# A routed-attention and SwiGLU kernel: the fifth head group's transposition moves from TensorE to VectorE, with loads and mask rows reordered

## The chip, the core and the metric

The kernel runs on one core of a Trainium2 chip. A core has TensorE (matrix products, written PE in the profile, its weight loads PEld), VectorE (DVE), ScalarE (ACT), GpSimd (POOL) and SyncE (SP), which here only issues DMA transfers. Each engine works through its own list of instructions in order and waits for the others by semaphores. Engines compute on SBUF, the on-chip memory of 128 partitions; TensorE writes to PSUM[...]. The metric is the device time of one execution in microseconds (us), the median of several runs.

## The reference

Inputs are q, k and v of shape (4 batches, 8 heads, 768 rows, 64), 16 centroids per head, and the weights of a gated feed-forward layer (512 to 1536 to 512), all in float32.

```python
q_assign = argmax(normalized(q) @ normalized(centroids).T)     # the cluster of each q row
k_assign = argmax(normalized(k) @ normalized(centroids).T)
mask = q_assign[:, :, :, None] == k_assign[:, :, None, :]
scores = where(mask, q @ k.T / sqrt(64), -1e9)
attn = softmax(scores)
x = (attn @ v) put together over heads                         # 3072 rows of 512
xn = x / sqrt(mean(x * x) + 1e-6) * rms_g
g, val = xn @ w_gate, xn @ w_val
out = (silu(g) * val) @ w_out
```

## The kernel before

**Mask inside the product.** The mask is never built. Each q and k row is extended from 64 to 80 numbers: 64 of data and 16 that are one at the row's own cluster and zero elsewhere (with a factor `ZS` = 2048 between data and mask). The product of two extended rows is then large where the clusters agree, and one exponential with an offset (`off`) does scale and mask together. The tiles `qext` and `kext` hold the extended rows with the 80 numbers on partitions; there are four of each, one per head group in flight.

**Groups and units.** The 32 heads (batch times head) are cut into eight *groups* of four heads (`HG`), group g being heads 4g to 4g + 3. The 3072 rows of attention and feed-forward are cut into eight *units* of 384 rows, two for each batch. Unit u attends over the two groups of its batch: units 0 and 1 use groups 0 and 1, units 2 and 3 groups 2 and 3, and so on. One unit has 8 heads times 3 steps, 24 *gaps*: in each, TensorE makes two score products (`s`, L345) and ScalarE exponentiates them into `pT` (L349). One step later TensorE multiplies `pT` with v into `acc` (L363), and for every second head VectorE divides (L368, L370) into `x`. There is a single `acc` bank.

**What is filled in between.** Behind the score products of each gap, `attention` pulls items from a list `fill` by weights that stand for their TensorE time, so that they are spread evenly over the gaps. In unit u the list holds: the last eight products of the gated layer of unit u - 2; the normalization of unit u - 1 (`rms`), with the DMA transposition of `xn` to `xnT` (L403, on the SP queue); the output rows of unit u - 2 (`o`, L466, 3 rows of three parts, stored from `o_sb` tiles); the preparation of group u + 2 (`group_work`); and the first sixteen products `gate` and `val` (L441) of unit u - 1, followed by Tanh on ScalarE (L449) and two VectorE operations (L450, L454). In unit 1 two groups are prepared, 2 and 3.

**Preparing a group.** For each head: q and k are loaded (L85 or L93) into one of six `qk` stage buffers, transposed so that the 64 numbers lie on partitions (`trans`, into `qkT`, three tiles of two heads), cast to bf16 into `qext` and `kext` (`cast`, L237), and v is loaded into one of eight `vs` buffers and cast to `vbf` on GpSimd (L240). Then, once for q and once for k of the whole group (`cluster_steps`): products with the centroids (`sc`, L251), a VectorE transposition (`scT`), maximum, comparison (`ohT`) and transposition back (`oh`). `place` (L294) then copies the mask rows of `oh` into partitions 64 to 79 of `qext` and `kext` with 16 small DMAs, eight for q, eight for k.

**Two ways to transpose.** The constant `BG` decides. For groups below `BG`, a load is one DMA of 192 KB, whole rows; TensorE transposes (`tq`, L218, three for each of q and k of a head), ScalarE evicts from PSUM (L224), and `kext` is cast by VectorE. For groups from `BG` on, a load of q or k is four DMAs of 48 KB, half rows of 32 numbers (128 bytes), put down so that 32x32 blocks turned in place give the whole transposition; VectorE does it in one instruction (L214) and `kext` is cast by GpSimd. There the factor `ZS` goes into the mask rows of k (L282) instead of k itself.

**Queues.** The order on each engine is the order in which the program emits, set by the code (no scheduler moves it). SP issues loads, x transpositions, stores and, for group 2, the mask rows, and stands still when the next one has to wait. GpSimd issues the weight loads (`wg`, `wv`, `wo`) and the mask rows of groups 3 to 7 between its casts. The loads of head n + `NQ` (6) and of v for head n + `NV` (8) are emitted by `others`, behind the v cast of head n.

Of the kernel before, what the change touches and what calls it, by code (L numbers as in the profile page):

```python
# [9 lines left out]
F32 = mybir.dt.float32  # L10
# [12 lines left out]
def kernel(  # L23
# [12 lines left out]
    nc = tc.nc  # L36
    B, H, S, D = q.shape
# [3 lines left out]
    P = 128  # L41
    ST = S // P
    HT = ST // 2
    UQ = HT * P
    HG = 4
# [8 lines left out]
    CUT = 2 * FC - 8  # L54
    LEAD = 6
    NQ, NV = 6, 8
    BG = 5

    ctx.enter_context(tc.manual_schedule())
    pool = lambda n, b, **kw: ctx.enter_context(tc.tile_pool(name=n, bufs=b, **kw))  # L60
# [7 lines left out]
    gate = pool("gate", 3)  # L68
    outp = pool("outp", 3)
# [7 lines left out]
    def src(a, n):  # L77
        b, h = divmod(n, H)
        return a[b, h].rearrange("(p t) d -> p t d", t=ST)

    def load(n, part, on=None):
        if n not in staged:
            staged[n] = stage.tile([P, 2, ST, D], F32, tag="qk", name="qk")
        if n < BG * HG:
            (on or nc.sync).dma_start(out=staged[n][:, part], in_=src((q, k)[part], n))  # L85
            return

        to = staged[n][:, part].rearrange("p t d -> p (t d)").rearrange("p (i r d) -> p i r d", i=HT, d=32)
        of = (q, k)[part][n // H, n % H].rearrange("(r p i e) (c d) -> e c p i r d", p=32, i=HT, e=2, d=32)
        for e in range(2):  # L90
            for c in range(2):
                r = 32 * (2 * e + c)
                nc.sync.dma_start(out=to[r:r + 32], in_=of[e, c])  # L93

    def load_qk(n):
        if n < B * H:
            load(n, 0)
            load(n, 1)

    def load_v(n, vq=None):  # L100
        if n >= B * H:
            return
        stagedv[n] = stage.tile([P, ST, D], F32, tag="vs", name="vs", bufs=NV)
        (vq or nc.sync).dma_start(out=stagedv[n], in_=src(v, n))
# [104 lines left out]
    def trans(g, h, part, on=None):  # L209
        if (g, h // 2) not in qkT:  # L210
            qkT[g, h // 2] = qk32.tile([P, 2, 2, UQ], F32, tag="qkT", name="qkT")
        qk = staged[g * HG + h]
        if g >= BG:
            nc.vector.transpose(qkT[g, h // 2][:, h % 2, part], qk[:, part].rearrange("p t d -> p (t d)"))  # L214
            return
        ps = ps_g.tile([P, UQ], F32, tag="gen", name="tq")
        for i in range(HT):
            nc.tensor.transpose(ps[:, i * P:(i + 1) * P], qk[:, part, 2 * i:2 * i + 2].rearrange("p t d -> p (t d)"),  # L218
                                ident_f)
        to, by = qkT[g, h // 2][:, h % 2, part], 1.0 / ZS if part else 1.0  # L220
        if on is nc.vector:
            nc.vector.tensor_scalar_mul(to, ps, by)  # L222
        else:
            nc.scalar.activation(to, ps, ACT.Copy, scale=by)  # L224
# [5 lines left out]
    def cast(on, g, h, part, es=(0, 1)):  # L230
        for e in es:
            to = cols((kext if part else qext)[g % 4][:D, h], g, e)
            of = qkT[g, h // 2][e * D:(e + 1) * D, h % 2, part]
            if on is nc.scalar:
                nc.scalar.copy(to, of)
            else:
                on.tensor_copy(to, of)  # L237

    def vcast(n):
        nc.gpsimd.tensor_copy(vbf[n // HG % 4][:, n % HG, :, :D], stagedv[n])  # L240
# [24 lines left out]
    def cluster_steps(g, m):  # L265
# [13 lines left out]
        def back():  # L279
            put[g, m] = asg.tile([P, UQ], BF16, tag="oh", name="oh", bufs=3)  # L280
            if m and g >= BG:
                nc.vector.tensor_scalar_mul(of["ohT"], of["ohT"], ZS)  # L282
# [6 lines left out]
    def place(on, g, m, es=(0, 1)):  # L289

        ext = (kext if m else qext)[g % 4]
        for h in range(HG):
            for e in es:
                on.dma_start(out=ext[D:D + NC, h, e * UQ:(e + 1) * UQ],  # L294
                             in_=put[g, m][32 * h + e * NC:32 * h + (e + 1) * NC])
# [39 lines left out]
    def scores(u, h, i):  # L335
# [12 lines left out]
        of = ps[:, :, :w] if nt == HT else flat[:, :n * w].rearrange("p (c w) -> p c w", w=w)  # L348
        nc.scalar.activation(pT[u, h][:, n * i:n * i + n, :w], of, ACT.Exp, bias=off, scale=scale if g >= BG else scale * ZS)  # L349

# [107 lines left out]
    def out_rows(u, t):  # L458
        b, col, _ = UNITS[u]
        return out[b * S:(b + 1) * S].rearrange("(p t) f -> p t f", t=ST)[:, (col + t) % HT * 2 + (col + t) // HT]  # L460
# [11 lines left out]
    def out_part(u, t, i):  # L472

        c = slice(*((0, DM // 2), (DM // 2, DM * 3 // 4), (DM * 3 // 4, DM))[i])
        to = ps_g.tile([P, c.stop - c.start], F32, tag="gen", name="o")
        for f in range(FC):
            nc.tensor.matmul(to, lhsT=gvT[u][:, f, t * P:(t + 1) * P], rhs=wo[:, f, c], start=f == 0, stop=f == FC - 1)  # L477
        o = outp.tile([P, c.stop - c.start], F32, tag="o_sb", name="o_sb")
        if i == 1:
            nc.vector.tensor_copy(o, to)  # L480
        else:
            nc.scalar.copy(o, to)
        nc.sync.dma_start(out=out_rows(u, t)[:, c], in_=o)


    def group_work(g):

        t, c = [], []
        for h in range(HG):
            n = g * HG + h  # L490
            w = 0.0 if g >= BG else 0.3
            t += [(w, lambda h=h: trans(g, h, 0)), (w, lambda h=h: trans(g, h, 1))]

            def others(n=n):
                vcast(n)
                load_qk(n + NQ)
                load_v(n + NV)

            def both(h=h, f=others):
                cast(nc.gpsimd, g, h, 0)  # L500
                f()
                cast(nc.gpsimd if g >= BG else nc.vector, g, h, 1, (0,))
            if g == 2:
                c.append((0.0, others))
            else:
                c += [(0.0, both), (0.0, lambda h=h: cast(nc.gpsimd if g >= BG else nc.vector, g, h, 1, (1,)))]
        a = []
        for m in range(2):
            a += [(0.0 if i else 0.7, f) for i, f in enumerate(cluster_steps(g, m))]
            if g == 3:  # L510
                a.append((0.0, lambda m=m: place(nc.gpsimd, g, m)))
            elif g == 2:
                a.append((0.0, (lambda: (place(nc.sync, g, 1), place(nc.sync, g, 0, (1,)))) if m else
                          (lambda: place(nc.sync, g, 0, (0,)))))
        if g > 3:
            a[:1] = [(1.4, lambda f=(a[0][1], a.pop(4)[1]): [x() for x in f])]
            a.append((0.0, lambda: [place(nc.gpsimd, g, m) for m in range(2)]))
        return t, c, a
# [5 lines left out]
    def group(g):  # L524

        if g >= NG:
            return [], []
        t, c, a = group_work(g)
        return [x for h in range(HG) for x in t[2 * h:2 * h + 2] + c[2 * h:2 * h + 2]], a
# [77 lines left out]
    def second_batch():  # L607
        nc.sync.dma_start(out=hold, in_=invs[0].rearrange("p a t -> p (a t)"))
        for n in range(H + HG, H + NQ):
            load_qk(n)  # L610
        for n in range(H, H + NV):
            load_v(n)

    def gap1():
# [61 lines left out]
    for u in range(1, NU):  # L676
        ffn, o, g = ffn_work(u - 1), out_work(u - 2) if u > 1 else [], u + 2
        if u == 1:
            t, c, a = group_work(2)
            t3, c3, a3 = group_work(3)  # L680
            n = LEAD - 4
            o3 = [(0.0, lambda i=i: load_o(i)) for i in range(0, FC, 4)]
            prep = c + a + spread(weave(t3[n:], c3), o3) + a3[:5]
            idle = const.tile([P, 1], BF16)

            def norm():
                rms(0)
                nc.gpsimd.tensor_copy(idle, xn[0][:, CC - 1, HT - 1, P - 1:])
                for h in range(HG):
                    casts(pool_, H + h, K0, Q0, K1, Q1)  # L690

            hooks = {(1, 0, 0): late[6], (1, 0, 1): lambda: (late[7](), norm())}
            hooks.update({(1, *divmod(2 + i, HT)): t3[i][1] for i in range(n)})
            hooks[1, *divmod(LEAD - 1, HT)] = lambda: xtrans_all(0)
            fill = spread(ffn[:CUT], prep)
            attention([(1, h) for h in range(H)], fill, LEAD, hooks)
        else:
            fill = ffn_work(u - 2)[CUT:] + [(0.0, lambda u=u: rms(u - 1))]
            rows, clusters = group(g)
            if u == 2:  # L700
                fill += spread(o[:3], [(0.0, f) for _, f in a3[5:]])
                o = o[3:]
            fill += spread(o, rows) + spread(ffn[:CUT], clusters)
            attention([(u, h) for h in range(H)], fill, 1 if g < NG else 0)
# [41 lines left out]
```

The softmax here doesn't subtract the row's maximum and nothing guards it: scores larger than these inputs give would overflow.

## Time and profile before

| | |
|---|---|
| time, median of 3 runs | 333.88 us (333.72 to 334.36) |
| span of the profiled run | 331.7 us |
| score products `s`, L345 | 384, mean 328 ns |
| `gate` and `val`, L441 | 384 each, mean 326 ns |
| output products `o`, L466 | 276, mean 379 ns |
| TensorE transpositions `tq`, L218 | 120, mean 277 ns |
| exponentials, L349 | 192, mean 904 ns |
| VectorE transpositions `qkT`, L214 | 24, mean 544 ns |
| small q and k loads, L93 | 96 of 48 KB, median 2.7 us to landing |
| large q and k loads, L85 | 38 of 192 KB, medians 4.1 and 4.2 us to landing |

The profile is of one execution. A page gives the busy time of each engine, the chain of work that ended last, and groups of instructions by line; the trace behind it gives waits (who waited for whom: total, times, longest) and timelines (start, duration, engine, line, what; an idle time before and its releaser in brackets). Matmuls overlap, so a group's durations add up to more than the time that it takes; the distance from start to start shows that time. TensorE's clock was granted in full all through.

### The profile page before, as it was taken

Reading aid. Unit: us, or ns where it says so; the run is one execution under the profiler, and the core shown is the slowest. Engines: PE = TensorE matmul, PEld = TensorE weight load, DVE = VectorE, ACT = ScalarE, POOL = GpSimd, SP = SyncE. Lnnn points to the kernel's source line nnn. Section 1 sums busy time; section 2 is a strip of 40 time slices with the busy share of each in tenths; the row PEclk is TensorE's granted clock in tenths of the full one; section 3 lists DMA queues with packets and bytes.
Section 4 is the critical chain, followed back from the end, with each engine's and each line's share of the span. In section 5 each row is a group of like instructions: output and inputs, shape, how many; then the busy total and the mean of one; then the engine's idle time right before and its main releaser. Section 6 shows DMA issues by size and latency. Waiting matters only on the chain.

```text
span 331.7 us, 7838 instructions
## 1 busy us (share of the span) xinstructions
PE 323.6 (98%) x2901; PEld 195.4 (59%) x2901; DVE 222.1 (67%) x507; ACT 250.5 (76%) x437; POOL 124.7 (38%) x249
## 2 busy tenths in 40 slices
PE   8999899999999999999999999999999999999996
PEld 4647557565656655665556655665566656655654
DVE  6999876868378694877678694876355644685430
ACT  5899979976878877798768876798788868863322
POOL 6999498240926338260834438270000000000000
PEclk9999999999999999999999999999999999999999
DMA  8999988956755625561550022000400040002002
GB/s 272 374 262 203 244 161 224 204 152 127 154 118 98 146 55 117 118 137 34 90 139 26 14 60 85 3 21 4 121 24 1 2 109 35 2 1 77 20 0 97
DMA packets 71269, 34.23 MB, mean 103 GB/s; under 512 B 51392, under 2 KB 68160, under 8 KB 71232
## 3 DMA queue, kind: packets, MB, share of 16 engines
q1 hardware_dynamic: 62576, 27.64, 31.8%
q0 software_dynamic: 8368, 5.71, 10.5%
q8 instruction: 23, 0.38, 0.5%
q10 hardware_dynamic: 288, 0.39, 0.4%
q14 instruction: 14, 0.11, 0.1%
HBM read 28.61 MB, written 6.29 MB: 105 GB/s over the span
## 4 chain that ended last, share of the span: by engine, by line
PE 80%; DVE 10%; ACT 6%; issue 2%; DMA 1%; ACTq 0%; DVEq 0%
PE gate L441 17%; PE o L466 17%; PE val L441 17%; PE s L345 15%; PE acc L363 8%; ACT pT L349 3%; PE sc L251 2%; PE tq L218 1%; ACT xn L390 1%; DVE xn L400 1%; DVE kext L329 1%; DVE qext L329 1%; DVE pads L324 1%; ACT th L449 1%; PE o L477 1%
## 5 line engine op out<-in xcount | busy, mean ns | idle before, releaser
L349 ACT ACTIVATE pT<-s,off 128x768 bf16<-128x768 f32 x192 | 170.9, 904 | 31.8 <-PE s L345 31.3
L345 PE MATMUL s<-qext,kext 80*128 80x384 bf16 x384 | 94.9, 328 | 2.4 <-ACT pT L349 1.6
L441 PE MATMUL gate<-xnT,wg 128*128 128x384 bf16 x384 | 78.3, 326 | 0.1
L441 PE MATMUL val<-xnT,wv 128*128 128x384 bf16 x384 | 78.1, 326 | 0.0
L450 DVE SCALAR_TENSOR_TENSOR th<-th,gate 128x384 f32<-128x384 f32 x84 | 46.2, 550 | 37.2 <-ACT th L449 36.6
L466 PE MATMUL o<-wo,gvT 128*128 128x512 bf16 x276 | 68.1, 379 | 0.0
L345 PEld LDWEIGHTS <-kext 80*128 80x128 bf16 x384 | 36.4, 98 | 35.9 <-issue 9.3
L454 DVE SCALAR_TENSOR_TENSOR gvT<-th,val 128x384 bf16<-128x384 f32 x84 | 46.4, 553 | 9.7 <-PE val L441 3.0
L449 ACT ACTIVATE th<-gate 128x384 f32<-128x384 f32 x84 | 41.1, 490 | 15.0 <-PE gate L441 14.3
L441 PEld LDWEIGHTS <-wg 128*128 128x128 bf16 x384 | 36.0, 97 | 23.0 <-issue 0.8
L363 PEld LDWEIGHTS <-pT 128*128 128x128 bf16 x1152 | 43.4, 97 | 10.0 <-DVE x L370 1.0
L441 PEld LDWEIGHTS <-wv 128*128 128x128 bf16 x384 | 36.0, 97 | 22.5
L237 POOL CAST qext<-qkT 64x384 bf16<-64x384 f32 x64 | 36.0, 568 | 35.2 <-DVE inv L368 20.8
L363 PE MATMUL acc<-vbf,pT 128*128 128x65 bf16 x1152 | 45.7, 193 | 0.6 <-ACT pT L349 0.2
L466 PEld LDWEIGHTS <-gvT 128*128 128x128 bf16 x276 | 25.8, 97 | 25.6 <-issue 0.6
L294 POOL DMA_DIRECT2D qext<-oh x40 | 19.1, 487 | 34.8 <-DVE oh L283 29.0
L237 POOL CAST kext<-qkT 64x384 bf16<-64x384 f32 x46 | 25.4, 552 | 3.7 <-DVE qkT L222 2.1
L294 POOL DMA_DIRECT2D kext<-oh x40 | 19.2, 489 | 18.9 <-DVE oh L283 18.9
L469 ACT COPY o_sb<-o 128x512 f32<-128x512 f32 x23 | 13.5, 585 | 16.1 <-PE o L466 16.1
L368 DVE RECIPROCAL inv<-acc 128x6 f32<-128x6 f32 x32 | 6.0, 189 | 21.6 <-PE acc L363 21.2
L218 PE MATMUL tq<-ident_f,qk 128*128 128x128 f32 x120 | 18.9, 277 | 0.1
L370 DVE TENSOR_TENSOR x<-acc,inv 128x384 f32<-128x384 f32 x32 | 17.8, 557 | 1.1
(83 smaller groups left out, 241.0 us busy)
## 6 DMA issues: line engine op xcount, KB each, us to landing
vs<-in_v_dram SPq DMA_DIRECT2D x32, 192.0 KB, 4.2
out_dram<-o_sb SPq DMA_DIRECT2D x23, 256.0 KB, 2.7
qk<-in_q_dram SPq DMA_DIRECT2D x20, 192.0 KB, 4.1
qk<-in_k_dram SPq DMA_DIRECT2D x18, 192.0 KB, 4.2
qk<-in_q_dram SPq DMA_DIRECT2D x48, 48.0 KB, 2.7
qk<-in_k_dram SPq DMA_DIRECT2D x48, 48.0 KB, 2.7
wg<-in_moe_w_gate_dram POOLq DMA_DIRECT2D x4, 384.0 KB, 8.5
wv<-in_moe_w_val_dram POOLq DMA_DIRECT2D x4, 384.0 KB, 10.7
```

The lines of the kernel that those rows point to most:

```text
L218: nc.tensor.transpose(ps[:, i * P:(i + 1) * P], qk[:, part, 2 * i:2 * i + 2].rearrange("p t d -> p (t d)"), ident_f)
L237: on.tensor_copy(to, of)
L294: on.dma_start(out=ext[D:D + NC, h, e * UQ:(e + 1) * UQ], in_=put[g, m][32 * h + e * NC:32 * h + (e + 1) * NC])
L345: nc.tensor.matmul(ps[:, j, :w] if nt == HT else flat[:, j * w:(j + 1) * w], lhsT=cols(kext[g % 4][:KR, hh], g, kc // HT, kc % HT * P, (kc ...
L349: nc.scalar.activation(pT[u, h][:, n * i:n * i + n, :w], of, ACT.Exp, bias=off, scale=scale if g >= BG else scale * ZS)
L363: nc.tensor.matmul(acc[:, h % 2, t], lhsT=pT[u, h][:, kc, t * P:(t + 1) * P], rhs=vbf[g % 4][:, hh, kc % HT * 2 + kc // HT], start=kc == 0 ...
L370: nc.vector.tensor_tensor(dst, acc[:, :, :nt, :D], inv[:, :, :nt].unsqueeze(3).broadcast_to([P, 2, nt, D]), op=ALU.mult)
L441: nc.tensor.matmul(ps, lhsT=w[:, c, f * P:(f + 1) * P], rhs=xnT[u][:, c, :n], start=c == 0, stop=c == CC - 1)
L449: nc.scalar.activation(th, ps, ACT.Tanh, scale=0.5)
L450: nc.vector.scalar_tensor_tensor(th, th, 1.0, ps, op0=ALU.add, op1=ALU.mult)
L454: nc.vector.scalar_tensor_tensor(gvT[u][:, f, :n], gates[u], 0.5, ps, op0=ALU.mult, op1=ALU.mult)
L466: nc.tensor.matmul(outs[u], lhsT=gvT[u][:, f, t * P:(t + 1) * P], rhs=wo[:, f], start=f == 0, stop=f == FC - 1)
```

## The change

Five edits go together. `BG` falls from 5 to 4: group 4 (heads 16 to 19, prepared in unit 2) is loaded in half rows and transposed by VectorE like the groups after it, which takes 24 transpositions from TensorE. The first two heads of groups 5, 6 and 7 (`LATE`) are no longer loaded by `others` but in the unit before their group's preparation, right after the normalization has emitted its x transposition, so that SP doesn't have them ahead of it. v is loaded four heads ahead (`AV`) instead of eight, still with eight buffers. The mask rows of group 2 are issued by GpSimd instead of SP. And the three last store pieces take their tiles from the `gate` pool instead of `outp`.

```diff
-    BG = 5
+    AV = 4
+    LATE = [n for n in range(20, B * H) if n % HG < 2]
+    BG = 4
...
-        o = outp.tile([P, c.stop - c.start], F32, tag="o_sb", name="o_sb")
+        o = gate.tile([P, UQ], F32, tag="th", name="o_sb")[:, :c.stop - c.start]
...
                 vcast(n)
-                load_qk(n + NQ)
-                load_v(n + NV)
+                if n + NQ not in LATE:
+                    load_qk(n + NQ)
+                load_v(n + AV)
...
             elif g == 2:
-                a.append((0.0, (lambda: (place(nc.sync, g, 1), place(nc.sync, g, 0, (1,)))) if m else
-                          (lambda: place(nc.sync, g, 0, (0,)))))
+                a.append((0.0, (lambda: (place(nc.gpsimd, g, 1), place(nc.gpsimd, g, 0, (1,)))) if m else
+                          (lambda: place(nc.gpsimd, g, 0, (0,)))))
...
-        for n in range(H, H + NV):
+        for n in range(H, H + AV):
             load_v(n)
...
             rows, clusters = group(g)
+            fill += [(0.0, lambda n=n: load_qk(n)) for n in LATE if n // HG == u + 3]
```

## The prediction

> **What bounds the kernel now.** I read three views, from coarse to fine. First the page: which engine is full, and which holds the chain that ended last.
>
> ```profile
> PE 323.6 (98%) x2901; PEld 195.4 (59%) x2901; DVE 222.1 (67%) x507; ACT 250.5 (76%) x437; POOL 124.7 (38%) x249
> ...
> PE 80%; DVE 10%; ACT 6%; issue 2%; DMA 1%; ACTq 0%; DVEq 0%
> ```
>
> TensorE is busy for 323.6 of 331.7 us and holds 80% of the chain. Second, TensorE's own waits between 78 and 296 us, most of units 2 to 7 (a unit is half a batch's rows):
>
> ```profile
> PE s L345 <- ACT pT L349: 0.5, 2, 0.3
> ```
>
> That is all: 0.5 us in 218. Here, TensorE work that goes away comes off the end, and a new wait adds to it. Third, the timeline of unit 2, where the change puts its hand (start, duration with overlap, engine, line):
>
> ```profile
> 79.37 0.49 PE L345 MATMUL s<-qext,kext 80*128 80x384 bf16 x2
> 79.70 1.16 PE L218 MATMUL tq<-ident_f,qk 128*128 128x128 f32 x6
> 80.69 1.03 PE L466 MATMUL o<-wo,gvT 128*128 128x512 bf16 x4
> 81.56 0.49 PE L345 MATMUL s<-qext,kext 80*128 80x384 bf16 x2
> 81.89 0.49 PE L218 MATMUL tq<-ident_f,qk 128*128 128x128 f32 x3
> 82.22 1.02 PE L466 MATMUL o<-wo,gvT 128*128 128x512 bf16 x4
> ...
> 83.95 0.53 PE L218 MATMUL tq<-ident_f,qk 128*128 128x128 f32 x3
> 84.31 1.03 PE L466 MATMUL o<-wo,gvT 128*128 128x512 bf16 x4
> ...
> 85.51 0.82 PE L218 MATMUL tq<-ident_f,qk 128*128 128x128 f32 x6
> 86.16 0.49 PE L345 MATMUL s<-qext,kext 80*128 80x384 bf16 x2
> ...
> 87.36 0.49 PE L218 MATMUL tq<-ident_f,qk 128*128 128x128 f32 x3
> 87.68 0.49 PE L345 MATMUL s<-qext,kext 80*128 80x384 bf16 x2
> ...
> 89.42 0.49 PE L218 MATMUL tq<-ident_f,qk 128*128 128x128 f32 x3
> 89.75 0.49 PE L345 MATMUL s<-qext,kext 80*128 80x384 bf16 x2
> 90.08 0.81 PE L441 MATMUL gate<-xnT,wg 128*128 128x384 bf16 x4
> ```
>
> The 24 `tq` are the fifth group's transpositions (group 4, heads 16 to 19), in a stream without holes. What each costs is read from its start to the next start, not from the duration.
>
> **What the Trainium skill says.** "VectorE: DVE Perf Modes", section "The three transpose paths": TensorE turns a whole 128x128 into PSUM, VectorE only 32x32 blocks. So VectorE can take this over only if the load has put the blocks in place: hence the half rows. The trace agrees that both exist: 272 ns for one TensorE transposition, 535 for a VectorE 128x384. "DMA: Bandwidth & Descriptors", section "Issuing engines are not separate DMA queues", says that another issuing engine saves only the sequencer's time; the trace gives 484 ns on GpSimd against 560 to 588 on SP (medians), so moving the mask rows matters for what stands behind them. The same page, "Anatomy of one DMA", says that semaphore waits are taken by the issuing sequencer. The trace agrees: SP stands 96.8 us in total before the x transposition (L403).
>
> **The change part by part.**
>
> *Fifth group by VectorE (BG 5 to 4).* TensorE loses the 24 `tq`. Start to next start: 0.99, 0.33, 0.36, 0.65, 0.32, 0.33, together 2.98 us. Streaming alone is less: 6 in 0.65 is 108 ns each, 24 of them 2.6. Most of the rest is the first piece's wait for a PSUM bank, which the chain puts on VectorE's `scT`; an output row that has its bank takes its place, so this should go too. I take 2.95. ScalarE loses 8 evictions of 0.49 us, off the path.
>
> VectorE gets 8 transpositions x 0.535 = 4.3 us and a scaling of 0.25; it loses 8 `kext` casts x 0.355 = 2.8. Net +1.8 on 26.5 busy of 38. Unit 3 carries this load already (8 `qkT` at L214, 26.9 of 37 busy) with TensorE at 36.74 of 37. In the built order seven transpositions, 3.7 us, stand ahead of the reciprocal that frees the only `acc` bank. They can start when `oh` is done at 82.6 and end at 86.4; the reciprocal ran at 88.76, and by my count of the new order its matmuls end near 87. GpSimd gets 8 casts x 0.5 on 17.7 of 38, for heads used in unit 4. On the path: nothing.
>
> *A race that the gain tightens.* In the middle of unit 2 the scores pass to group 3, whose `kext` mask rows GpSimd sends at 82.90, as soon as `oh` is there:
>
> ```profile
> 82.90 3.99 POOL L294 DMA_DIRECT2D kext<-oh x8 [11.76 <-DVE oh L283]
> ```
>
> These eight land after 1.9, 2.5 and 3.4 us (least, median, most): the first at 85.4, and its scores are the ones at 86.16. Slack 0.76. In the built order of the changed kernel, from the `sc` products (75.11) to those scores, there are 7 output parts x 0.864, 5 score pairs x 0.33, 2 `acc` x 0.55 and the products' 0.78: 9.6 us, so 84.7. The `oh` chain hardly moves: ScalarE's squares ahead of it follow a score pair that I count at 73.2 instead of 73.5, with a gate's work less between, so 0 to 0.6 earlier. Rows sent at 82.3 to 82.9 land at 84.2 to 86.3. TensorE waits 0 to 1.6 us; I take 0.4.
>
> *The loads.* Group 4's eight q and k loads become 32 pieces of 0.62 us, 20 us of SP instead of 8 x 0.43. They are wanted near 82. Before, SP issued the last two heads at 69.6 to 71.7, having stood behind `vs` slots that wait for GpSimd's casts (10.5 us in one piece) and behind the mask rows (55.8 to 69.5). Both go: v runs four ahead on eight buffers, so its slot is free early. My sum: second batch done at 36, heads 14 and 15 at 38, then 4 x 5 us and v: near 63, landed (2.7 us) near 66. Sixteen us of room.
>
> *Two heads behind the x transposition.* Without this the gain would not arrive. Before:
>
> ```profile
> 81.54 2.63 SPq L93 DMA_DIRECT2D qk<-in_k_dram  x4
> 84.27 0.57 SPq L104 DMA_DIRECT2D vs<-in_v_dram  x1
> 85.02 1.99 SPq L403 DMA_TRANSPOSE xnT<-xn  x1
> ```
>
> xn was ready at 79.77, the transposition went at 85.02 behind heads 20 and 21, and landing takes 3.7 to 4.8 us: 88.7 to 89.8. The first gate that reads it began at 90.08. With 3 us less ahead that gate would have waited. Now SP is free at 79.8: landed by 84.6, wanted at 87. The stores behind the two heads come 10 us later, but an output buffer is wanted again only three rows on. Cost and gain: nothing.
>
> *Mask rows of group 2 on GpSimd.* 16 x 0.484 = 7.7 us, behind casts that end at 50.5: done near 58.3, landed near 61. Unit 2's first scores come at 65.9 (0.75 us after the pair before, so perhaps the rows on SP were just late there: up to 0.4 to gain; I take none). GpSimd works in order: behind the rows stand group 3's casts (1.6 us a head) and the three `wo` loads, issued before at 52.3, 57.3 and 60.9, now at 59.9, 63.8 and 66.1. At 8.5 us to landing: 68.4, 72.3, 74.6. Output matmuls want them at 74.2, 75.9 and 77.9 by the new order. Least room: 3.3 us. If the rows crawl at the 0.86 us each that they took on SP (13.7 us), the last `wo` comes 2.7 too late. The nearest row, group 3's first eight at 67.3, took 0.484; I take no cost.
>
> *Last pieces in gate tiles.* The last copy began at 328.59, 0.11 after its matmuls' end: 0 to 0.1 to gain.
>
> Sum: 333.88 - 2.95 + 0.4 = 331.3.
>
> **The rivals.**
>
> *About half lost.* For: the mask rows at their worst (1.6 us) do this alone; so would VectorE's burst if it starts late. Against: unit 3 runs with such a burst and no hole. 333.88 - 2.95 + 1.6 = 332.5.
>
> *No difference, `wo` late.* For: GpSimd's queue grows by 7.7 us ahead of it. Against: 3.3 us of room, and SP's small pieces leave the DMA less loaded than the 1.1 of 56 to 66 us. With the rows at 0.86 us: 331.3 + 2.7 = 334.0.
>
> *Slower.* For: 24 more issues in 128-byte runs join weights and v between 36 and 60 us, where the DMA stood at 1.2 of its time. If the small pieces hold up unit 1's loads or the x transposition by 5 us: 331.3 + 5 = 336.3. Against: v's four heads (0.75 MB) leave this stretch, and no TensorE wait on a load shows there now.
>
> **How the numbers follow.** Forecast 0.77 (330.6 to 331.9), half lost 0.11, no difference 0.05, slower 0.07. The low end, 330.5, is all 2.95 and 0.4 at unit 2's start with the rows in time; the high end, 332.5, the worst of the mask rows. Some 0.15 lies above, 0.05 below. Faster by over 0.2% (below 333.2): 0.77 + 0.11 = 0.88; within: 0.04; slower: 0.08.
>
> **What would show it.** Right: no `tq` after unit 1, TensorE's count at 2877 and busy near 321; eight transpositions by VectorE in unit 2 that wait for no load; the x transposition within 1 us of xn; 16 rows on GpSimd in 8 us. A TensorE hole of 0 to 1.6 us near 85, before the first scores of group 3. Wrong: an output matmul near 76 waiting for `wo`, the first gate for `xnT`, `acc` for VectorE, or unit 2 shorter by 3 while another unit grows.

## The result and the profile after

The changed kernel took 331.74 us (median of four runs, 331.38 to 332.73) against 334.09 (333.72 to 334.36) for the kernel before beside it: 0.9935 of the time, 95% interval 0.9911 to 0.9960. A second set of four runs gave 331.95, ratio 0.9922 (0.9908 to 0.9937). The forecast was 331.3 us, with 330.5 to 332.5 as the range.

The page of the changed kernel, its lines of busy time and of the chain:

```profile
PE 320.9 (97%) x2877; PEld 192.8 (58%) x2877; DVE 223.7 (68%) x508; ACT 247.8 (75%) x429; POOL 136.3 (41%) x273
...
PE 77%; DVE 10%; ACT 6%; SPq 3%; issue 2%; DMA 1%; POOL 0%; DVEq 0%; ACTq 0%; POOLq 0%
```

TensorE has 24 matmuls and 2.7 us less, VectorE 1.6 us more, GpSimd 11.6 more. The span falls by 2.1 us, 331.7 to 329.6. (Line numbers are two higher than before in the functions concerned.) The waits of TensorE's products between 76 and 294 us are still those for exponentials alone (the view lists idle times over 0.15 us):

```profile
PE s L347 <- ACT pT L351: 0.8, 3, 0.3
```

Its timeline in the middle of unit 2, where the transpositions stood:

```profile
82.59 1.03 PE L468 MATMUL o<-wo,gvT 128*128 128x512 bf16 x4
83.46 0.49 PE L347 MATMUL s<-qext,kext 80*128 80x384 bf16 x2
83.79 1.03 PE L468 MATMUL o<-wo,gvT 128*128 128x512 bf16 x4
84.84 0.50 PE L347 MATMUL s<-qext,kext 80*128 80x384 bf16 x2
85.17 1.03 PE L468 MATMUL o<-wo,gvT 128*128 128x512 bf16 x4
86.04 0.49 PE L347 MATMUL s<-qext,kext 80*128 80x384 bf16 x2
86.37 0.71 PE L365 MATMUL acc<-vbf,pT 128*128 128x65 bf16 x18
86.91 0.81 PE L443 MATMUL gate<-xnT,wg 128*128 128x384 bf16 x4
```

No `tq` is left. Four output parts take 0.86 us from start to next start; the one at 83.79 takes 1.05, so a hole of 0.19 us stands ahead of the first scores of group 3 at 84.84. (A hole is counted here from start to start: what the distance is longer than usual. The waits view counts from the modelled end of the product before, and so gives up to 0.2 us less.) What ended this one shows on TensorE's weight loads, which take the mask rows' tile `kext` first:

```profile
PEld L347 <- DMA kext<-oh: 0.5, 1, 0.5
```

The first gate comes at 86.91 instead of 90.08.

Where the 2.1 us come from, by the start of each unit's first scores: unit 2 takes 38.67 us instead of 41.46, 2.79 less. Units 0 and 1 and 4 to 7 agree within 0.04. Unit 3 takes 37.59 instead of 37.38: its second scores now wait for an exponential (0.43 us of pause instead of 0.22), as units 4 and 5 did all along. The *tail*, from the end of the last product to the end of the span, is 3.73 instead of 3.19 us. Start-up was 0.09 shorter. So -2.79 + 0.21 + 0.54 - 0.09, with rounding -2.1.

### The profile page after: what moved, and what is told of

It reads as the page before. It is cut to its first block, busy times and chain, and to the rows that moved or that the text cites. A ratio compares the mean times of both kernels' runs of the same rounds, so it can differ in the third digit from the quotient of the medians.

```text
span 329.6 us, 7822 instructions
## 1 busy us (share of the span) xinstructions
PE 320.9 (97%) x2877; PEld 192.8 (58%) x2877; DVE 223.7 (68%) x508; ACT 247.8 (75%) x429; POOL 136.3 (41%) x273
## 4 chain that ended last, share of the span: by engine, by line
PE 77%; DVE 10%; ACT 6%; SPq 3%; issue 2%; DMA 1%; POOL 0%; DVEq 0%; ACTq 0%; POOLq 0%
PE o L468 18%; PE gate L443 15%; PE val L443 15%; PE s L347 15%; PE acc L365 8%; ACT pT L351 3%; SPq L95 3%; PE sc L253 2%; DMA qk<-in_k_dram 1%; ACT xn L392 1%; ACT th L451 1%; DVE kext L331 1%; DVE qext L331 1%; PE warm L131 1%; DVE pads L326 1%
## 5 line engine op out<-in xcount | busy, mean ns | idle before, releaser
L296 POOL DMA_DIRECT2D qext<-oh x48 | 23.1, 491 | 27.0 <-DVE oh L285 22.5
L239 POOL CAST kext<-qkT 64x384 bf16<-64x384 f32 x54 | 29.4, 545 | 4.0 <-DVE qkT L224 2.2
L296 POOL DMA_DIRECT2D kext<-oh x48 | 23.0, 488 | 14.7 <-DVE oh L285 14.6
L242 POOL CAST vbf<-vs 128x384 bf16<-128x384 f32 x32 | 16.6, 527 | 1.6
```

The costliest lines, as they stand in the source:

```text
L296: on.dma_start(out=ext[D:D + NC, h, e * UQ:(e + 1) * UQ], in_=put[g, m][32 * h + e * NC:32 * h + (e + 1) * NC])
```

## The experiments

Every time is set beside runs of the kernel before on the same chip, and the ratio is given with its 95% interval.

**The order edits without the fifth group's move.**

```diff
 # the changed kernel
-    BG = 4
+    BG = 5
```

> The changed kernel with BG = 5: all the order edits, group 4 by TensorE as before. Theory: without the 24 transpositions gone there is nothing to gain, since TensorE did not wait for loads before: 333.7 to 334.1, as before. Rival: earlier loads and x transposition are worth something of their own: 333.0 or less.

Measured: 334.34 us, ratio 0.9991 (0.9980 to 1.0002). Unit 2 takes 41.47 us, as before within 0.01, and the first piece of `tq` still has its pause of 0.29 us. Loads that come earlier are worth nothing by themselves; the gain is the 24 transpositions.

**The fifth group's move without the order edits.**

```diff
 # the kernel before
-    BG = 5
+    BG = 4
```

> The kernel before with BG = 4 alone: group 4 in half rows and by VectorE, all queues as before. Theory (the gain is TensorE's 24 transpositions, and the order of the loads is what lets it arrive): SP stands behind v slots and the mask rows until about 69.5 as before, and has 20 us of small pieces to issue, some of them ahead of the mask rows of group 2 and the rest ahead of the x transposition. Mask rows of group 2 about 10 us later than before, x transposition near 92 or later instead of 85, so TensorE waits some 5 to 10 us in unit 2: 337 to 342 us, slower than before. Rival (the order edits are ornament, only BG matters): 331.5 to 332 as the whole change.

Measured: 356.21 us, ratio 1.0643 (1.0595 to 1.0690): the theory's direction, and nearly three times the largest loss that it allowed. TensorE's waits between 60 and 120 us:

```profile
PE gate L441 <- DMA xnT<-xn: 10.3, 1, 10.3
PE s L345 <- DMA kext<-oh: 9.5, 2, 9.3
```

and SP's queue in that stretch:

```profile
69.90 0.58 SPq L104 DMA_DIRECT2D vs<-in_v_dram  x1
70.58 2.47 SPq L294 DMA_DIRECT2D qext<-oh  x4
73.14 4.96 SPq L294 DMA_DIRECT2D kext<-oh  x8
...
104.25 0.56 SPq L104 DMA_DIRECT2D vs<-in_v_dram  x1
104.99 1.93 SPq L403 DMA_TRANSPOSE xnT<-xn  x1
```

The mask rows of group 2 went at 73.14 instead of 58.47, behind the pieces of heads 16 and 17, and unit 2 began 9.8 us late (74.97 instead of 65.15). The x transposition went at 104.99 instead of 85.02. Both feared waits came, one after the other: 19.8 us. The rest is a slower clock around each hole's end (a granted 0.50 for 10.24 us from 69.49 and again from 103.62; more on this below) and a longer tail (5.54 us).

**Each order edit taken back alone.** First, heads 20 and 21 ahead of the x transposition again:

```diff
-    LATE = [n for n in range(20, B * H) if n % HG < 2]
+    LATE = []
```

> The changed kernel with LATE empty: heads 20 and 21 are loaded ahead of the x transposition again, all else kept. The prediction said that without this edit the gain would not arrive. Theory as the prediction put it: transposition behind about 10 us of small pieces, landed some 5 us later than in the changed kernel (84), near 89, first gate wanted at 87: TensorE waits about 2 us, 333.5. Rival, from the changed kernel's SP timeline (free from 71.3 to 79.3): heads 20 and 21 go in that free time for the most part, the transposition goes near 82, lands near 86, nobody waits: 331.7 to 332.0.

Second, v eight heads ahead again:

```diff
-    AV = 4
+    AV = 8
```

> The changed kernel with v again eight heads ahead on eight buffers: SP waits for GpSimd's casts of v to free a buffer (before: 12.0 us in all). Theory: SP stands until about 50 for the cast of head 8, then issues heads 14 to 19, the last near 77 to 80; the transposition of the last head by VectorE wants it near 84, so up to 1 us is lost: 331.7 to 332.7. Rival (v ahead is needed as much as the rest): heads 18 and 19 after 85 and VectorE's burst stands with acc behind it, 2 us or more: 333.7 or more.

Third, the mask rows of group 2 on SP again:

```diff
-                a.append((0.0, (lambda: (place(nc.gpsimd, g, 1), place(nc.gpsimd, g, 0, (1,)))) if m else
-                          (lambda: place(nc.gpsimd, g, 0, (0,)))))
+                a.append((0.0, (lambda: (place(nc.sync, g, 1), place(nc.sync, g, 0, (1,)))) if m else
+                          (lambda: place(nc.sync, g, 0, (0,)))))
```

> The changed kernel with the mask rows of group 2 on SP again. Theory: rows go at about 54 to 67 behind heads 16 and 17, the first k rows land at 60 to 65, just before unit 2's first scores at 65.9; heads 18 and 19 follow to about 79, the x transposition goes near 80: 0 to 1 us lost, 331.7 to 332.7. Rival (the rows hold up unit 2): first scores of unit 2 wait 3 us or more, 334.7 or more.

| | time, us | ratio to before | x transposition issued at | first gate waited |
|---|---|---|---|---|
| the change | 331.74 | 0.9935 (0.9911 to 0.9960) | 79.28 | 0 |
| v eight ahead | 334.35 | 1.0001 (0.9980 to 1.0021) | 84.79 | 3.1 us |
| rows on SP | 335.08 | 1.0020 (0.9996 to 1.0044) | 85.35 | 2.3 us |
| no LATE | 338.31 | 1.0123 (1.0099 to 1.0147) | 87.08 | 3.4 us |

Each of the three taken back alone is enough to lose the whole gain. I had expected that the edits stand in for one another, and that is refuted: the waiter is the same each time, and the transposition's place on SP is what all three protect. (The rivals' times came with v eight ahead and with the rows on SP, but not the waiters that they named.) The two right-hand columns are of one profiled execution each, and these were among the longer ones: 335.87 us with v eight ahead, the longest of twelve, 337.71 with the rows on SP, and 338.94 without LATE. TensorE's long wait with LATE empty, between 80 and 100 us, is this line, with 3.1 and 2.3 in its place for the other two (the race for group 3's mask rows adds 0.3 at most):

```profile
PE gate L443 <- DMA xnT<-xn: 3.4, 1, 3.4
```

SP of the changed kernel, and below it of the one with LATE empty, show how little room there is:

```profile
69.31 1.97 SPq L106 DMA_DIRECT2D vs<-in_v_dram  x3
79.28 1.55 SPq L405 DMA_TRANSPOSE xnT<-xn  x1
```

```profile
73.06 3.89 SPq L95 DMA_DIRECT2D qk<-in_q_dram  x4
76.99 3.23 SPq L95 DMA_DIRECT2D qk<-in_k_dram  x4
80.32 0.56 SPq L106 DMA_DIRECT2D vs<-in_v_dram  x1
80.98 2.59 SPq L95 DMA_DIRECT2D qk<-in_q_dram  x4
83.61 2.63 SPq L95 DMA_DIRECT2D qk<-in_k_dram  x4
86.34 0.56 SPq L106 DMA_DIRECT2D vs<-in_v_dram  x1
87.08 1.87 SPq L405 DMA_TRANSPOSE xnT<-xn  x1
```

In the change SP has 8 us to spare before xn is ready; two heads of small pieces took 13.3 us here (73.06 to 86.34), more than the 10.5 that 0.62 us a piece, with the load of v between them, makes.

**Why a wait costs more than it lasts.** With LATE empty, unit 2 takes 6.64 us more than in the change, while the hole is 3.6 us. The windows of that kernel's TensorE (busy us, granted clock, DMA share, GB/s):

```profile
84.00:88.00 4.00, 3.50 (x33) 1.00 0.63 105
88.00:92.00 4.00, 0.76 (x3) 0.77 0.90 211
92.00:96.00 4.00, 4.00 (x21) 0.50 0.47 74
96.00:100.00 4.00, 4.00 (x45) 0.87 0.71 168
```

The granted clock is 0.50 for 6.8 us from 90.18, 1.1 us before the hole ends, and in 92 to 96 us TensorE runs 21 matmuls, where the change runs 28 long ones or over 40 mixed ones in such a window. From the hole's end (91.2) to 97.0 half the time is lost, 2.9 us: 3.6 + 2.9 is nearly all of the 6.6. In the profiles with v eight ahead and with the rows on SP it is 3.41 us at half clock. The Trainium skill names this: "TensorE: Matmul & The Clock Gate", section "Why this matters for your kernels", advises against idle gaps of TensorE over some 3 us between bursts of products, or the clock falls back to half. The traces agree on the half clock and roughly on the length: holes of 2.45, 3.2 and 3.6 us halved it, one of 2.60 (next experiment) did not. Nor does the same kernel always do the same. With v eight ahead the profiled execution had a mean granted clock of 0.995 over the span, the other eleven 0.997 to 1.000; the median loss there, 2.2 us by the ratios, is no more than the wait. So no fixed length can be read off here.

**The mask rows of group 3 sent in the opposite order of heads.**

```diff
-        for h in range(HG):
+        for h in (range(HG)[::-1] if (g, m) == (3, 1) else range(HG)):
             for e in es:
                 on.dma_start(out=ext[D:D + NC, h, e * UQ:(e + 1) * UQ],
```

> The changed kernel with the k mask rows of group 3 sent in the opposite order of heads, so that the head used first gets its rows 6 x 0.48 = 2.9 us later. Theory (the first scores of group 3 are a race that has no slack left, the hole of 0.19 us at 84.8): a hole of about 3 us there, and 3 us or a little more on the time: 334.7 to 335.7. Rival (the 0.19 us has another cause, the rows have slack): under 1.5 us on the time, 333 or less.

Measured: 334.43 us, ratio 1.0025 (1.0001 to 1.0049). TensorE's waits between 80 and 100 us:

```profile
PE s L347 <- DMA kext<-oh: 2.4, 1, 2.4
```

The hole ahead of group 3's first scores is 2.60 us instead of 0.19, 2.4 more for 2.9 us of delay; so the race is real and at its edge in the change. The weight loads wait 2.9 us for these rows. Unit 2 is longer by 2.41 us, all of it this hole, and the time, by 2.7 (3.0 by the ratios), is about what I had expected. In five of the twelve executions the mean granted clock was 0.990 to 0.995 and the time 335.7 to 338.2 us, so there this hole seems to have halved the clock too; they were not profiled.

**Group 3's cluster work all in unit 1.**

```diff
-            prep = c + a + spread(weave(t3[n:], c3), o3) + a3[:5]
+            prep = c + a + spread(weave(t3[n:], c3), o3) + a3
...
             if u == 2:
-                fill += spread(o[:3], [(0.0, f) for _, f in a3[5:]])
-                o = o[3:]
+                pass
```

> The changed kernel with all of group 3's cluster work in unit 1, so that its k mask rows are there long before unit 2 needs them. Theory: the hole of 0.19 us goes, and with it the wait for the VectorE chain at the start of unit 2; unit 1 has VectorE and ScalarE enough (31 of 42 and 36 of 42 us busy before): 331.5, 0.2 better than the change at most 0.4. Rival: unit 1 becomes too full for VectorE and exponentials wait: 332 or more.

Measured: 331.54 us (330.64 to 331.92), ratio 0.9911 (0.9895 to 0.9928). The hole is gone and units 1 and 2 together take 70.49 us instead of 70.72; in the total 0.2 us can't be told apart from none.

**The tail.** Two experiments on the last 3 us. The last pieces in `outp` tiles again:

```diff
-        o = gate.tile([P, UQ], F32, tag="th", name="o_sb")[:, :c.stop - c.start]
+        o = outp.tile([P, c.stop - c.start], F32, tag="o_sb", name="o_sb")
```

> The changed kernel with the last store pieces in outp tiles again. In the profiled run of the change the last product ends 2.62 us earlier than before, but the end of the span is 3.73 us behind it instead of 3.19. Theory: this 0.5 us is how the last store happened to land, not the gate tiles; their edit is worth 0 to 0.1: same as the changed kernel within 0.2 us, 331.7 (331.5 to 332.0). Rival: the gate tiles cost the 0.5 us: 331.2.

Measured: 333.44 us (331.52 to 334.37), ratio 0.9953 (0.9931 to 0.9975): outside what I had expected, and too scattered to rank against the change; why isn't known. Its trace shows what the edit does: the last copy starts 0.41 us after the last product instead of 0.04, having waited for an older store to leave its `outp` tile. The tail stays long (3.65 us), so the gate tiles are not its cause.

What differs stands in the view of DMA from 325 us on. The change, and below it the same kernel in its second profile:

```profile
q1 hardware_dynamic: 522, 0.41, 28.0%
q8 instruction: 1, 0.02, 1.2%
issues: line engine op xcount, KB each, median us to landing
out_dram<-o_sb SPq DMA_DIRECT2D x1, 128.0 KB, 3.0
out_dram<-o_sb SPq DMA_DIRECT2D x2, 64.0 KB, 2.4
```

```profile
q1 hardware_dynamic: 534, 0.44, 32.8%
issues: line engine op xcount, KB each, median us to landing
out_dram<-o_sb SPq DMA_DIRECT2D x1, 128.0 KB, 1.7
out_dram<-o_sb SPq DMA_DIRECT2D x2, 64.0 KB, 1.5
```

I take `q8 instruction` for a fetch of 16 KB of TensorE's own instructions: there are 23 in a run, one for some 250 of TensorE's recorded products and weight loads. In the change's first profile the last one began 0.08 us before the last product ended, and the stores landed after 2.4 and 3.0 us; in its second there was none and they landed after 1.5 and 1.7 us, with a tail of 3.09 us. Before, it began 4.75 us ahead of the last product's end.

All fourteen traces fall in line. In five (the change, v eight ahead, rows reversed, rows early, `outp`) the last fetch began within 0.1 us of the last product's end, and the tail is 3.65 to 3.77 us. In three (the fifth group's move alone, no LATE, rows on SP) it began 0.9 to 1.0 us before that end, and the tail is 4.0 to 5.5. In the other six it began 1.5 us or more before, or only after the last store, and the tail is 3.09 to 3.20. With the 24 transpositions in place (before, and the order edits alone) it came 4.7 and 5.4 us ahead, with just these 24 gone within 1.1 us, but for the change's second profile, where it came 4.8 us behind. So taking instructions from TensorE moved it into the last stores, though not in every execution. The second execution was not faster for its short tail: its device time was 331.86 us, against 331.38 for the first, and 2.9 us of it lay outside the span instead of 1.8. The late fetch began there, 1.75 us behind the span's end; whether the execution waited for it isn't shown.

To test it, sixteen instructions more at the start (eight products and eight weight loads):

```diff
-    WARM = 7
+    WARM = 6
...
                              rhs=warm.unsqueeze(1).broadcast_to([P, 4, P]), start=True, stop=True)
+        for i in range(9 if first else 0):
+            nc.tensor.matmul(to[:, :32], lhsT=warm, rhs=warm[:, :32], start=True, stop=True)
```

> The changed kernel with sixteen more TensorE instructions at the start (one warm-up product of 512 columns less, nine of 32 more), nothing else. In the trace of the change a 16 KB fetch of TensorE's instructions starts 0.1 us before its last product ends and the last stores land late; before, with sixteen instructions more, it started 4.7 us ahead of the end. Theory: the fetch shares a DMA engine with the last stores and makes the tail 3.7 instead of 3.2 us; now it moves back to some 4.7 us ahead and the tail to about 3.2: 0.5 us less than the changed kernel. Rival (the tail is longer for another reason): no change in the tail.

The change itself beside it:

> The changed kernel unaltered, to have it beside the next ones on the same chip: 331.7 (331.4 to 332.5), with the last store landing 2.5 us after the last product and the span ending some 3.7 after it.

Measured: 331.25 us (330.83 to 331.45), ratio 0.9898 (0.9884 to 0.9913), against 331.95 (331.86 to 332.21), 0.9922 (0.9908 to 0.9937), for the change on the same chip. The tail is 3.20, and the fetch now began 1.55 us ahead of the end, not 4.7: sixteen is by how much the recorded instructions of all engines together had fallen (7838 to 7822), while TensorE alone had lost 24 products and 24 weight loads, so sixteen bring the fetch only part of the way back. The four runs lie below all four of the change, but the intervals of the ratios overlap a little, and the change's profile beside it had a short tail too (3.09 us): a gain is likely, not certain, and how much of the 0.7 us is the tail's isn't shown.

Group 3's early cluster work and the sixteen instructions in one kernel:

> Both small mends together: group 3's cluster work all in unit 1, and the sixteen instructions. Theory: 0.2 and 0.5 us less than the changed kernel, 331.0; the fastest of all here. Rival: they do not add: 331.5 or more.

Measured: 331.15 us (331.08 to 331.56), ratio 0.9900 (0.9885 to 0.9914): no better than the sixteen instructions alone. The 0.2 us of the early rows is below what this can show.

**One group more by VectorE.**

```diff
-    BG = 4
+    BG = 3
```

> The changed kernel with BG = 3: group 3 too in half rows and by VectorE, another 24 transpositions (2.6 us) off TensorE. Theory: SP's issuing is what ends it. Heads 12 to 15 need 20 to 30 us more of SP between 33 and 79 us, where the changed kernel was at it without a break to 71, so heads 14 and 15 come late for unit 1 and the x transposition of unit 1 goes near 100 instead of 79: TensorE waits 10 us or more, 340 to 355. Rival: the room in DMA and SP is enough and another 2.6 us come off: 329.

Measured: 341.14 us, ratio 1.0186 (1.0117 to 1.0255). Unit 1 did gain: 30.53 us instead of 32.05. But TensorE's waits between 60 and 100 us, and below them GpSimd's between 50 and 90, are not those that I had named, so the time fell into my range of 340 to 355 for another reason:

```profile
PE o L468 <- DMA wo<-in_moe_w_out_dram: 7.3, 2, 5.0
PE s L347 <- ACT pT L351: 0.3, 1, 0.3
```

```profile
POOL vbf L242 <- DMA vs<-in_v_dram: 7.5, 2, 4.5
```

SP's queue is still the root: the v loads of heads 14 and 15 go at 64.21 and 72.03 behind small pieces. GpSimd waits for them with its casts, the `wo` loads stand behind those casts (62.46, 71.20 and 79.55 instead of 59.95, 64.07 and 66.66), and the output matmuls wait for `wo`. The x transposition was late too (89.05), but after these holes nobody waited for it. The granted clock was 0.50 here for 3.41 us from 77.16 and for 6.83 from 83.99.

## Why the prediction was right

*The 24 transpositions, 2.95 us.* Unit 2 shrank by 2.79, which contains the new hole of 0.19: 2.98 without it. That is the forecast's streaming (2.6) and the first piece's wait together. With the order edits alone nothing moved, so this is the whole of the gain.

*The race for group 3's mask rows, 0 to 1.6, taken 0.4.* The rows went at 82.25 (forecast 82.3 to 82.9), the scores wanted them at 84.65 (forecast 84.7), the hole was 0.19 us. The reversed order shows that it is this race.

*VectorE's burst.* Seven transpositions ran from 81.88 to 85.17; the reciprocal behind them came at 87.11 and waited 1.95 us for its matmuls, not the other way round. It cost nothing.

*The loads.* The sum for SP was too short: the last pieces were out at 69.2, not near 63, because head 16's eight pieces, beside weights and v, took 11.7 us (35.70 to 47.37) instead of the 5 a head that the sum had. Group 4's data were early enough all the same, with less room than the sixteen us of the forecast.

*Two heads behind the x transposition.* Without this, the gain would not arrive: right, with 338.3 us as the proof. The same holds for v and the mask rows, which the prediction had only as helpers of the loads. The price of a late transposition there was the wait alone; the half clock after it was not in it.

*Mask rows of group 2 and `wo`.* Rows from 50.37 to 58.33, `wo` at 59.95, 64.07 and 66.66, landing 7.0 to 8.4 us: as forecast, no wait. The possible 0.4 us at unit 2's start was no row's: the pause of 0.42 us is still there, and its releaser is the exponential.

*Sum.* Forecast -2.55, measured -2.35 and -2.44 in the times of the two sets, and in the spans of the two profiles -2.1 and -2.65. What was missing is +0.21 us at the start of unit 3 and, in the first profile, where the fetch falls on the stores, some 0.5 us of tail. Neither was among the terms. That the forecast lay within 0.7 us of both medians owes little to luck, since its main term came out within 0.03 us. One thing was luck: the hole ahead of group 3 was 0.21 us smaller than taken, and unit 3 grew by just that. The gate tiles were valued at 0 to 0.1 and the trace of before showed no wait there. With `outp` tiles in the changed kernel the last copy came 0.4 us later, but in that profile the end did not move with it.

*The rivals.* None came. "Half lost", by the rows at their worst, is what reversing their order makes and more: a hole of 2.60 us. `wo` late appears only with one group more.

## What to carry to other kernels

When the bounding engine is freed of work, look at who feeds it next: each transfer that was just in time is late by what was gained. Here the gain was some 2.4 us and hung on one DMA's place in an in-order queue, and any of three small edits taken back lost it all. Put what a critical transfer waits for into the queue in the order of need, and count the issue time of small pieces at the rate of a busy stretch, not of a quiet one.

## What the runs showed of the hardware

In the profiled executions a TensorE hole of 2.45 to 3.6 us ahead of the gates came with 3.4 to 6.8 us at a granted clock of 0.50, beginning from 1.1 us before the hole's end to 1.1 us after it, so that the loss was up to 1.8 times the hole; with v eight ahead eleven of twelve executions kept a mean clock of 0.997 or more. And where a 16 KB fetch of instructions began up to 1.0 us before the last product ended, the last stores landed late: after medians of 2.4 and 3.0 us instead of 1.5 and 1.7 in two executions of the same kernel, with the end of the span some 0.6 us later. Whether fetch and stores shared a DMA engine isn't known, and in these two the device time did not follow the span.
